# Fold and Newton step of the row norms on GpSimd, and a new order of VectorE's work within each pair

## The chip, the cores and the metric

The kernel runs on one core of one Trainium2 chip. The metric is the device time of one execution in microseconds (us). The core has five engines that work side by side, each through its own queue in order: TensorE (PE; its weight loads are shown apart as PEld), VectorE (DVE), ScalarE (ACT), GpSimd (POOL) and SyncE (SP), whose queue here issues the loads from memory. An instruction that waits for a semaphore holds up everything behind it in its own queue.

## The reference

```python
def rmsnorm(x, g):
    rms = np.sqrt(np.mean(x * x, axis=-1, keepdims=True) + 1e-06)
    return x / rms * g
q_n, k_n = rmsnorm(q, g_q), rmsnorm(k, g_k)         # (8, 12, 448, 64)
scores = q_n @ k_n^T / sqrt(64)
attn = softmax(scores) ; o = attn @ v               # heads joined: x is (3584, 768)
h = x @ w_in                                        # (3584, 1024)
solu = h * softmax(h)
ln = (solu - mean) / sqrt(var + 1e-06) * g_ln
out = ln @ w_out                                    # (3584, 768)
```

Eight sequences of 448 tokens with 12 heads of 64 go through attention with normalised q and k; the result goes through a feed-forward block of width 1024. The two weight matrices arrive as 64-bit floats and are turned into 32-bit floats on the chip.

## The kernel before

Work goes by pairs of heads: N = 48 pairs, n = 0 to 47, six to a sequence. The main loop (it begins after `load(3)` and `begin(0)`) runs over the pairs, and in the turn n it does pieces of several of them at once:

- **scores** (L598, L601): `scores(n, kc)` for kc = 0 to 3, each two halves of matmuls into PSUM tile `s`, and an exponential on ACT into `E`. The ring of `s` has two buffers, so the matmuls of a chunk wait for the exponential two chunks earlier.
- **values and sums** of the pair before: `values(n-1)` (L626, tile `o`) and `sums(n-1)` (L637, tile `sm`), the row sums of `E` by a matmul with ones. `add` forms the sums `es` that this matmul reads: for n < 12 two DVE additions (L612); from n = 12 one GpSimd addition (L615) and two DVE additions on top (L617).
- **divide(n-1)** (L650, L651, L652, L654): DVE turns the sums round, takes reciprocals and multiplies, which frees the buffers of `o` and `sm`. Its result goes to `xT`.
- **the norms of coming pairs**: `squares(n+3)` on ACT (L537), `row_sums(n+3)` on DVE (L542), `swap_sums(n+3)` (four GpSimd copies, L551), `fold_sums` (L555), `rsqrt_seed(n+2)` (three short ACT steps, L562 to L564), `rsqrt_step(n+2)` (a Newton step of three instructions on 128x28 elements, L568 to L570), `normalise(n+2)` on GpSimd (L575, tile `qkn`, one buffer), `qk_transpose(n+1)` on DVE (L585, tile `qkT`) and `gain(n+1)` on ACT (L589).
- **weights**: `convert_w` of one or two of 28 pieces a turn up to n = 21, in four stages that `step()` issues: low bits on ACT (L464, L465), high bits on DVE (L468, L469), join on DVE (L473), and for `w_out` a product on ACT (L478). `load_next` loads the piece three further on into one of three buffers `raw` (L449); it needs the buffer that the high and low bits have read.
- **feed-forward**: from n = 13 one event a turn, and from n = 23 up to four: `ff_in` (L669, tile `h`, one buffer), `ff_transpose` (L713), `ff_out` (L724). `ff_max` (L679, L682), `ff_moments` (L687 to L697, with one GpSimd power L697) and `ff_norm` (L701) follow an `ff_in` some units later. The rest of the events run after the loop.

`unit(f)` issues a piece of PE's work and then whatever `later` has put off to that place. The order within each engine is the order of the code; no scheduler changes it. The names in a DVE row of the trace read out<-in.

Of the kernel before, what the change touches and what calls it, by code (L numbers as in the profile page):

```python
# [14 lines left out]
OP = AluOpType  # L15
# [351 lines left out]
def fast_path(  # L367
# [17 lines left out]
    nc = tc.nc  # L385
# [11 lines left out]
    W_IN = 12  # L397
# [47 lines left out]
    def load_w(step):  # L445
        src, _, c, cols = step
        n = cols.stop - cols.start
        raw = work.tile([P, n, 2], U32, tag="raw", name="raw", bufs=3)
        nc.sync.dma_start(  # L449
            raw.rearrange("p n t -> p (n t)"),  # L450
            src[c * P : (c + 1) * P, :].bitcast(U32)[:, 2 * cols.start : 2 * cols.stop],
        )
        return raw
# [62 lines left out]
    def load(n):  # L516
        b, hp = divmod(n, NP)
        h0 = 2 * hp
        d = st[n] = {}
        d["qk"] = loads.tile([P, 2, NB, 32], FP32, tag="qk", name="qk", bufs=3)  # L520
        for s, src in enumerate((q, k)):
            for g in range(4):
                nc.sync.dma_start(
                    d["qk"][g * 32 : g * 32 + 32, s],
                    src[b, h0 + g // 2].rearrange("(b t) (x d) -> x t b d", t=32, x=2)[g % 2],
                )
# [7 lines left out]
    def squares(n):  # L534
        d = st[n]
        d["sq"] = work.tile([P, 2 * NB, 32], FP32, tag="sq", name="sq", bufs=1)
        nc.scalar.activation(d["sq"], d["qk"].rearrange("p s b d -> p (s b) d"), AF.Square)  # L537

    def row_sums(n):
        d = st[n]  # L540
        d["part"] = small.tile([P, 2 * NB], FP32, tag="part", name="part")
        nc.vector.tensor_reduce(d["part"], d["sq"], AX, OP.add)  # L542
# [3 lines left out]
    def swap_sums(n):  # L546
        d = st[n]
        d["ss"] = small.tile([P, 2 * NB], FP32, tag="ss", name="ss")
        for g in range(4):
            o = g ^ 1  # L550
            nc.gpsimd.tensor_copy(d["ss"][g * 32 : g * 32 + 32], d["part"][o * 32 : o * 32 + 32])  # L551

    def fold_sums(n):
        d = st[n]
        nc.vector.tensor_tensor(d["ss"], d["ss"], d["part"], OP.add)  # L555

    def rsqrt_seed(n):

        d = st[n]
        d["x"] = small.tile([P, 2 * NB], FP32, tag="nx", name="nx")  # L560
        d["y"] = small.tile([P, 2 * NB], FP32, tag="ny", name="ny")
        nc.scalar.activation(d["y"], d["ss"], AF.Ln, scale=1.0 / D, bias=eps)  # L562
        nc.scalar.activation(d["x"], d["ss"], AF.Copy, scale=-0.5 / D, bias=-0.5e-6)
        nc.scalar.activation(d["y"], d["y"], AF.Exp, scale=-0.5)  # L564

    def rsqrt_step(n):
        x, y = st[n]["x"], st[n]["y"]
        nc.vector.tensor_tensor(x, x, y, OP.mult)  # L568
        nc.vector.tensor_tensor(x, x, y, OP.mult)
        nc.vector.scalar_tensor_tensor(y, x, 1.5, y, OP.add, OP.mult)  # L570

    def normalise(n):
        d = st[n]
        d["qkn"] = work.tile([P, 2 * NB, 32], FP32, tag="qkn", name="qkn", bufs=1)
        nc.gpsimd.tensor_tensor(  # L575
            d["qkn"],
            d["qk"].rearrange("p s b d -> p (s b) d"),
            d["y"].rearrange("p b -> p b ()").to_broadcast([P, 2 * NB, 32]),
            OP.mult,
        )  # L580
# [10 lines left out]
    def scores(n, kc):  # L591
        d = st[n]
        if kc == 0:
            d["E"] = work.tile([SP, NJ, 2, S], FP32, tag="E", name="E")
        s = ps_t.tile([SP, 2, 512], FP32, tag="t", name="s")
        for h in range(2):
            hh = slice(h * D, (h + 1) * D)
            nc.tensor.matmul(  # L598
                s[:, h, 0:S], d["qkT"][hh, 1, kc * SP : (kc + 1) * SP], d["qkT"][hh, 0, :], start=True, stop=True
            )  # L600
        nc.scalar.activation(d["E"][:, kc], s[:, :, 0:S], AF.Exp)  # L601
# [5 lines left out]
    def add(n, kc):  # L607
        d = st[n]
        two = n < W_IN
        if kc in (1, 3) and two:  # L610
            d["es", kc] = work.tile([SP, 2, S], FP32, tag="es", name="es")
            nc.vector.tensor_tensor(d["es", kc], d["E"][:, kc - 1], d["E"][:, kc], OP.add)  # L612
        elif kc == 1:
            d["es", 3] = work.tile([SP, 2, S], FP32, tag="es", name="es")
            nc.gpsimd.tensor_tensor(d["es", 3], d["E"][:, 0], d["E"][:, 1], OP.add)  # L615
        elif not two:
            nc.vector.tensor_tensor(d["es", 3], d["es", 3], d["E"][:, kc], OP.add)  # L617
# [127 lines left out]
    def unit(f):  # L745
        nonlocal now
        f()
        now += 1
        due = [x for x in todo if x[0] <= now]
        todo[:] = [x for x in todo if x[0] > now]  # L750
        for _, g in sorted(due, key=lambda x: x[0]):
            g()
# [7 lines left out]
    stages = []  # L760

    def load_next():
        if len(raws) < len(wq):
            raws.append(load_w(wq[len(raws)]))
# [13 lines left out]
    def step():  # L778
        for c in stages:
            c.pop(0)()  # L780
# [5 lines left out]
    def second(t, a, b):  # L786
        return [(W_OUT + 1, lambda: ff_transpose(t)), a, (W_OUT + 1, lambda: ff_out(t, 0)), b, (W_OUT + 1, lambda: ff_out(t, 1))]

    nothing = (0, None)
    for t in range(NT):  # L790
# [4 lines left out]
        if len(waiting) > (LAG if t < NT - 8 else 1):  # L795
            c, _, d, _, e = second(waiting.pop(0), nothing, nothing)
# [6 lines left out]
    N = B * NP  # L803
# [7 lines left out]
    with tc.manual_schedule():  # L811
        for n in range(2):
            squares(n)
            row_sums(n)
            swap_sums(n)
            fold_sums(n)
            rsqrt_seed(n)
            rsqrt_step(n)
            normalise(n)
            if n == 0:  # L820
                qk_transpose(0)
                gain(0)
        squares(2)
        row_sums(2)
        swap_sums(2)
        load(3)
        begin(0)
        at = 0
        for n in range(N):
            due = []  # L830

            while at < len(events) and len(due) < (4 if n > W_OUT else 1) and events[at][0] <= n:
                due.append(events[at][1])
                at += 1

            def ff(k):
                for f in due[len(due) * k // 3 : len(due) * (k + 1) // 3]:
                    unit(f)


            unit(lambda: scores(n, 0))
            if n:
                add(n - 1, 3)
            if n + 1 < N:
                qk_transpose(n + 1)
            if n + 2 < N:
                fold_sums(n + 2)
            unit(lambda: scores(n, 1))
            step()
            ring = "o"  # L850
            ff(0)

            if n:
                unit(lambda: values(n - 1))
            if n >= W_IN:
                add(n, 1)
            if n + 2 < N:
                rsqrt_seed(n + 2)
            if n + 3 < N:
                squares(n + 3)  # L860
            if n + 4 < N:
                load(n + 4)
            if n + 2 < N:
                rsqrt_step(n + 2)
                normalise(n + 2)
            if n + 3 < N:
                row_sums(n + 3)
            step()
            for _ in stages:
                load_next()  # L870
            if n:
                unit(lambda: sums(n - 1))
                later(1, lambda n=n: divide(n - 1))
            if n + 1 < N:
                load_v(n + 1)
            if n + 3 < N:
                swap_sums(n + 3)
            step()
            begin(n + 1)
            if n + 1 < N:  # L880
                gain(n + 1)
            ring = "t"
            ff(1)

            unit(lambda: scores(n, 2))
            unit(lambda: scores(n, 3))
            add(n, 1 if n < W_IN else 2)
            ring = "o"
            ff(2)
        add(N - 1, 3)  # L890
        unit(lambda: values(N - 1))
        unit(lambda: sums(N - 1))
        divide(N - 1)
        ring = "t"

        last = events[at:]
        assert len(last) > len(wq) + 1
        again = [load_w(wq[x]) for x in range(2)]
        for x, (_, f) in enumerate(last):
            unit(f)  # L900
            if x < len(wq):
                check_w(x, again[x])
                if x + 2 < len(wq):
                    again.append(load_w(wq[x + 2]))
            if x == len(wq) + 1:
                check_all()
        for _ in range(4):
            unit(lambda: None)
# [73 lines left out]
```

## Time and profile before

| what | value |
|---|---|
| three runs | 1070.37, 1071.86, 1073.26 us (median 1071.86) |
| the profiled execution | 1071.4 us, of which 1069.6 us are the span from its first to its last instruction |
| PE busy | 998.1 us (93%) |
| DVE busy | 623.6 us (58%) |
| ACT busy | 379.3 us (35%) |
| POOL busy | 232.1 us (22%) |
| SP queue (q1) | 58.23 MB in 230016 packets |

The page cuts the span into 40 slices and gives each engine's busy share of a slice in tenths. The timeline lists start, length, engine, line, operation and out<-in, with the idle time of the engine just before in brackets and what ended it. The list of waits has: engine, what waited, what it waited for, us in total, number of times, the longest. The length of a matmul group is from its first start to the modelled end of its last.

### The profile page before, as it was taken

Reading aid. Unit: us, or ns where it says so; the run is one execution under the profiler, and the core shown is the slowest. Engines: PE = TensorE matmul, PEld = TensorE weight load, DVE = VectorE, ACT = ScalarE, POOL = GpSimd, SP = SyncE. Lnnn points to the kernel's source line nnn. Section 1 sums busy time; section 2 is a strip of 40 time slices with the busy share of each in tenths; the row PEclk is TensorE's granted clock in tenths of the full one; section 3 lists DMA queues with packets and bytes.
Section 4 is the critical chain, followed back from the end, with each engine's and each line's share of the span. In section 5 each row is a group of like instructions: output and inputs, shape, how many; then the busy total and the mean of one; then the engine's idle time right before and its main releaser. Section 6 shows DMA issues by size and latency. Waiting matters only on the chain.

```text
span 1069.6 us, 10556 instructions
## 1 busy us (share of the span) xinstructions
PE 998.1 (93%) x3571; PEld 446.4 (42%) x3571; DVE 623.6 (58%) x1013; ACT 379.3 (35%) x645; POOL 232.1 (22%) x314
## 2 busy tenths in 40 slices
PE   2988878898899999999999999999999999999997
PEld 0332323233244444444444444444444444455554
DVE  3999988888874355545454555444555443556430
ACT  4777754565533233323323233223322322111110
POOL 3322334324321122212131222112221111000000
PEclk9999989898999999999999999999999999999999
DMA  7756643343221111111221211211110002043330
GB/s 150 159 124 135 122 97 85 67 96 78 39 43 41 41 40 41 41 26 40 50 54 35 47 32 29 52 41 41 41 40 9 24 25 82 35 133 113 118 119 34
DMA packets 234426, 70.10 MB, mean 66 GB/s; under 512 B 223600, under 2 KB 223608, under 8 KB 234360
## 3 DMA queue, kind: packets, MB, share of 16 engines
q1 hardware_dynamic: 230016, 58.23, 25.2%
q10 hardware_dynamic: 4344, 11.08, 2.6%
q8 instruction: 30, 0.49, 0.2%
q14 instruction: 36, 0.29, 0.1%
HBM read 58.27 MB, written 11.01 MB: 65 GB/s over the span
## 4 chain that ended last, share of the span: by engine, by line
PE 69%; DVE 17%; ACT 7%; issue 3%; SPq 1%; DMA 0%; POOL 0%; ACTq 0%; DVEq 0%
PE po L724 28%; PE h L669 23%; PE o L626 7%; PE s L598 7%; DVE part L542 2%; DVE qkT L585 2%; PE sm L637 2%; PE pu L713 2%; DVE es L612 2%; ACT E L601 1%; DVE es L617 1%; DVE tmp L473 1%; DVE tmp L469 1%; DVE w_in L473 1%; DVE ss L555 1%
## 5 line engine op out<-in xcount | busy, mean ns | idle before, releaser
L669 PE MATMUL h<-w_in,xT 128*128 128x512 f32 x672 | 302.2, 599 | 0.0
L724 PE MATMUL po<-w_out,uT 128*128 128x384 f32 x896 | 299.4, 490 | 2.1 <-ACT uT L714 2.1
L724 PEld LDWEIGHTS po<-w_out,uT 128*128 128x128 f32 x896 | 167.4, 190 | 134.9 <-issue 14.5
L598 PE MATMUL s<-qkT 64*112 64x448 f32 x768 | 181.2, 590 | 44.0 <-ACT E L601 29.6
L601 ACT ACTIVATE E<-s 112x896 f32<-112x896 f32 x192 | 165.6, 911 | 87.0 <-PE s L598 86.8
L669 PEld LDWEIGHTS h<-w_in,xT 128*128 128x128 f32 x672 | 123.9, 190 | 164.2 <-issue 158.8
L626 PE MATMUL o<-E,v 112*64 112x448 f32 x768 | 156.3, 549 | 2.6 <-ACT uT L714 2.6
L697 POOL TENSOR_TENSOR he<-he,mhalf 128x1 f32<-128x1 f32 x28 | 22.0, 785 | 485.7 <-DVE he L696 392.4
L598 PEld LDWEIGHTS s<-qkT 64*112 64x112 f32 x768 | 61.8, 180 | 153.9 <-issue 64.9
L617 DVE TENSOR_TENSOR es<-es,E 112x896 f32<-112x896 f32 x72 | 80.2, 1114 | 57.5 <-ACT E L601 55.6
L575 POOL TENSOR_TENSOR qkn<-qk,ny 128x896 f32<-128x896 f32 x48 | 83.2, 1733 | 127.8 <-issue 71.7
L725 ACT COPY y<-po 128x384 f32<-128x384 f32 x56 | 26.8, 479 | 230.9 <-PE po L724 224.3
L615 POOL TENSOR_TENSOR es<-E 112x896 f32<-112x896 f32 x36 | 76.6, 2128 | 143.5 <-ACT E L601 129.7
L715 DVE COPY uT<-pu 128x512 f32<-128x512 f32 x28 | 19.3, 690 | 149.5 <-ACT uT L714 86.9
L626 PEld LDWEIGHTS o<-E,v 112*64 112x64 f32 x768 | 51.3, 138 | 100.8 <-issue 85.1
L682 ACT ACTIVATE u<-h,hmax 128x1024 f32<-128x1024 f32 x28 | 31.2, 1113 | 160.2 <-DVE hmax L679 160.2
L679 DVE TENSOR_REDUCE hmax<-h 128x1 f32<-128x1024 f32 x28 | 34.3, 1223 | 80.9 <-PE h L669 80.9
L637 PE MATMUL sm<-es,ones 112*64 112x448 f32 x240 | 56.1, 564 | 11.4 <-DVE es L617 10.2
L542 DVE TENSOR_REDUCE part<-sq 128x28 f32<-128x896 f32 x48 | 52.0, 1083 | 8.4 <-ACT sq L537 7.8
L551 POOL COPY ss<-part 32x28 f32<-32x28 f32 x192 | 50.0, 260 | 21.2 <-DVE part L542 12.3
L585 DVE STREAM_TRANSPOSE qkT<-qkn 128x896 f32<-128x896 f32 x48 | 53.0, 1104 | 1.9 <-POOL qkn L575 1.9
L687 DVE TENSOR_TENSOR u<-h,u 128x1024 f32<-128x1024 f32 x28 | 34.3, 1224 | 31.5 <-ACT u L682 31.3
(66 smaller groups left out, 637.2 us busy)
## 6 DMA issues: line engine op xcount, KB each, us to landing
raw<-in_moe_w_in_dram SPq DMA_DIRECT2D x24, 512.0 KB, 4.1
raw<-in_moe_w_out_dram SPq DMA_DIRECT2D x32, 384.0 KB, 3.3
qk<-in_q_dram SPq DMA_DIRECT2D x192, 56.0 KB, 2.4
qk<-in_k_dram SPq DMA_DIRECT2D x192, 56.0 KB, 2.3
v<-in_v_dram SPq DMA_DIRECT2D x48, 224.0 KB, 3.1
out_dram<-y ACTq DMA_DIRECT2D x28, 384.0 KB, 2.3
grow<-in_g_q_dram ACTq DMA_DIRECT2D x2, 0.2 KB
grow<-in_g_k_dram ACTq DMA_DIRECT2D x2, 0.2 KB
```

Of the source, the lines that this page charges most:

```text
L542: nc.vector.tensor_reduce(d["part"], d["sq"], AX, OP.add)
L551: nc.gpsimd.tensor_copy(d["ss"][g * 32 : g * 32 + 32], d["part"][o * 32 : o * 32 + 32])
L575: nc.gpsimd.tensor_tensor(d["qkn"], d["qk"].rearrange("p s b d -> p (s b) d"), d["y"].rearrange("p b -> p b ()").to_broadcast([P, 2 * NB, ...
L585: nc.vector.transpose(d["qkT"].rearrange("p s t -> p (s t)"), d["qkn"].rearrange("p b d -> p (b d)"))
L598: nc.tensor.matmul(s[:, h, 0:S], d["qkT"][hh, 1, kc * SP : (kc + 1) * SP], d["qkT"][hh, 0, :], start=True, stop=True)
L601: nc.scalar.activation(d["E"][:, kc], s[:, :, 0:S], AF.Exp)
L615: nc.gpsimd.tensor_tensor(d["es", 3], d["E"][:, 0], d["E"][:, 1], OP.add)
L617: nc.vector.tensor_tensor(d["es", 3], d["es", 3], d["E"][:, kc], OP.add)
L626: nc.tensor.matmul(d["o"][h * D : (h + 1) * D, :], d["v"][:, h, kc], d["E"][:, kc, h], start=(kc == 0), stop=(kc == NJ - 1),)
L637: nc.tensor.matmul(d["sm"][h * D : (h + 1) * D, :], ones[0:SP, :], es[:, h], start=(i == 0), stop=(i == len(tiles) - 1),)
L669: nc.tensor.matmul(d["h"][:, hs], xTs[m][:, c, i * P : (i + 1) * P], w_in[:, c, hs], start=(c == 0), stop=(c == KD - 1))
L724: nc.tensor.matmul(po, d["uT"][:, c], w_out[:, c, hs], start=(c == 0), stop=(c == KF - 1))
```

## The change

Two things are done. The fold (one instruction a pair) and the Newton step go from DVE to GpSimd. [...] And the order in a turn of the loop becomes another: the weight pieces' high bits and join stand ahead of `qk_transpose`, the next loads of raw weights follow at once, the swap and the fold of pair n+3 stand straight behind its row sums, and GpSimd's part of `es` stands behind those.

```diff
     def fold_sums(n):
         d = st[n]
-        nc.vector.tensor_tensor(d["ss"], d["ss"], d["part"], OP.add)
+        nc.gpsimd.tensor_tensor(d["ss"], d["ss"], d["part"], OP.add)
...
     def rsqrt_step(n):
         x, y = st[n]["x"], st[n]["y"]
-        nc.vector.tensor_tensor(x, x, y, OP.mult)
-        nc.vector.tensor_tensor(x, x, y, OP.mult)
-        nc.vector.scalar_tensor_tensor(y, x, 1.5, y, OP.add, OP.mult)
+        nc.gpsimd.tensor_tensor(x, x, y, OP.mult)
+        nc.gpsimd.tensor_tensor(x, x, y, OP.mult)
+        nc.gpsimd.tensor_scalar(x, x, 1.5, None, OP.add)
+        nc.gpsimd.tensor_tensor(y, x, y, OP.mult)
...
         swap_sums(2)
+        fold_sums(2)
         load(3)
...
             if n:
                 add(n - 1, 3)
+            unit(lambda: scores(n, 1))
+            step()
+            step()
+            for _ in stages:
+                load_next()
             if n + 1 < N:
                 qk_transpose(n + 1)
-            if n + 2 < N:
-                fold_sums(n + 2)
-            unit(lambda: scores(n, 1))
-            step()
             ring = "o"
             ff(0)
...
-            if n >= W_IN:
-                add(n, 1)
             if n + 2 < N:
                 rsqrt_seed(n + 2)
...
             if n + 3 < N:
                 row_sums(n + 3)
+                swap_sums(n + 3)
+                fold_sums(n + 3)
+            if n >= W_IN:
+                add(n, 1)
             step()
-            for _ in stages:
-                load_next()
...
-            if n + 3 < N:
-                swap_sums(n + 3)
-            step()
             begin(n + 1)
```

PE's instructions stand in the same order as before. In the changed kernel every line from 571 on has moved down by one (L585 is L586 there, and so on).

DVE, one turn of the early loop (n = 3, attention and weights only), before; it begins with the two additions `es` of the pair before:

```order
L612 TENSOR_TENSOR es<-E 112x896 x2
L585 STREAM_TRANSPOSE qkT<-qkn 128x896
L555 TENSOR_TENSOR ss<-ss,part 128x28
L468 TENSOR_SCALAR tmp<-raw 128x512
L469 SCALAR_TENSOR_TENSOR tmp<-raw,tmp 128x512
L568 TENSOR_TENSOR nx<-nx,ny 128x28
L569 TENSOR_TENSOR nx<-nx,ny 128x28
L570 SCALAR_TENSOR_TENSOR ny<-nx,ny 128x28
L542 TENSOR_REDUCE part<-sq 128x28
L473 TENSOR_TENSOR w_in<-tmp 128x512
L650 STREAM_TRANSPOSE r<-sm 128x448
```

The same place in the changed kernel:

```order
L613 TENSOR_TENSOR es<-E 112x896 x2
L468 TENSOR_SCALAR tmp<-raw 128x512
L469 SCALAR_TENSOR_TENSOR tmp<-raw,tmp 128x512
L473 TENSOR_TENSOR w_in<-tmp 128x512
L586 STREAM_TRANSPOSE qkT<-qkn 128x896
L542 TENSOR_REDUCE part<-sq 128x28
L651 STREAM_TRANSPOSE r<-sm 128x448
```

The four short instructions are gone, the three weight instructions stand together ahead of the transpose, and the row sums follow the transpose.

GpSimd, one turn from n = 12 on, before, with the first row of the next; `he` is the power of `ff_moments`, which every second turn has:

```order
L697 TENSOR_TENSOR he<-he,mhalf 128x1
L615 TENSOR_TENSOR es<-E 112x896
L575 TENSOR_TENSOR qkn<-qk,ny 128x896
L551 COPY ss<-part 32x28 x4
L615 TENSOR_TENSOR es<-E 112x896
```

The same turn in the changed kernel:

```order
L698 TENSOR_TENSOR he<-he,mhalf 128x1
L568 TENSOR_TENSOR nx<-nx,ny 128x28
L569 TENSOR_TENSOR nx<-nx,ny 128x28
L570 TENSOR_SCALAR nx<-nx 128x28
L571 TENSOR_TENSOR ny<-nx,ny 128x28
L576 TENSOR_TENSOR qkn<-qk,ny 128x896
L551 COPY ss<-part 32x28 x4
L555 TENSOR_TENSOR ss<-ss,part 128x28
L616 TENSOR_TENSOR es<-E 112x896
```

Five short instructions have come in, and `es` has gone from the front of the turn to its end, behind the normalisation, the copies and the fold.

SP's queue, one early turn and the start of the next, before:

```order
L523 DMA qk<-in_q_dram 32x14x32 x4
L523 DMA qk<-in_k_dram 32x14x32 x4
L449 DMA raw<-in_moe_w_in_dram 128x1024
L532 DMA v<-in_v_dram 112x8x64
L523 DMA qk<-in_q_dram 32x14x32 x4
```

and in the changed kernel:

```order
L449 DMA raw<-in_moe_w_in_dram 128x1024
L523 DMA qk<-in_q_dram 32x14x32 x4
L523 DMA qk<-in_k_dram 32x14x32 x4
L532 DMA v<-in_v_dram 112x8x64
L449 DMA raw<-in_moe_w_in_dram 128x1024
```

The raw weights, which wait for DVE's high bits of this turn, are now issued ahead of the turn's q and k.

## The prediction

> **What bounds the kernel now.** First the page's slices of PE, a window of the early pairs and one behind them (columns: window, length, then busy us with count for PE, PEld, DVE, ACT, POOL; granted clock, DMA share, GB/s), and the list of PE's waits up to 134 us (first row) and from 134 to 325 us (the others):
>
> ```profile
> PE   2988878898899999999999999999999999999997
> 54.00:81.00 27.00, 24.42 (x120) 8.45 (x120) 26.20 (x46) 19.38 (x33) 7.84 (x15) 1.00 0.59 123
> 134.00:160.00 26.00, 19.43 (x74) 7.08 (x72) 22.17 (x33) 15.06 (x25) 9.84 (x12) 0.87 0.47 99
> PE s L598 <- ACT E L601: 15.8, 13, 4.0
> PE s L598 <- ACT E L601: 13.8, 7, 6.6
> PE sm L637 <- DVE es L617: 10.2, 4, 2.9
> ```
>
> From about the twelfth slice PE is full to the end: there nothing is to be had. Before that there are two stages with room: pairs without feed-forward up to 134 us (**stage A**), where DVE is busy 26.2 of 27 us, and pairs with one `ff_in` up to about 300 us (**stage B**), where PE waits and its granted clock falls to 0.87. One period of stage A, from the timeline:
>
> ```profile
> 79.45 1.09 DVE L542 TENSOR_REDUCE part<-sq 128x28 f32<-128x896 f32 x1
> 79.52 1.70 POOL L575 TENSOR_TENSOR qkn<-qk,ny 128x896 f32<-128x896 f32 x1 [6.22 <-issue]
> 80.45 1.31 DVE L473 TENSOR_TENSOR w_in<-tmp 128x512 uint32<-128x512 uint32 x1
> 80.67 0.65 ACT L589 ACTIVATE qkT<-qkT,gcol 128x448 f32<-128x448 f32 x1
> 81.22 1.70 ACT L601 ACTIVATE E<-s 112x896 f32<-112x896 f32 x2
> ...
> 83.86 2.08 DVE L612 TENSOR_TENSOR es<-E 112x896 f32<-112x896 f32 x2
> 83.92 3.23 PE L626 MATMUL o<-E,v 112*64 112x448 f32 x16
> 85.86 1.10 DVE L585 STREAM_TRANSPOSE qkT<-qkn 128x896 f32<-128x896 f32 x1
> 86.89 0.15 DVE L555 TENSOR_TENSOR ss<-ss,part 128x28 f32<-128x28 f32 x1
> 86.95 0.42 DVE L468 TENSOR_SCALAR tmp<-raw 128x512 uint32<-128x512 uint32 x1
> 86.97 1.67 PE L637 MATMUL sm<-es,ones 112*64 112x448 f32 x8
> 87.41 0.69 DVE L469 SCALAR_TENSOR_TENSOR tmp<-raw,tmp 128x512 uint32<-128x512 uint32 x1
> 88.02 0.18 DVE L568 TENSOR_TENSOR nx<-nx,ny 128x28 f32<-128x28 f32 x1
> 88.58 1.76 PE L598 MATMUL s<-qkT 64*112 64x448 f32 x8
> 88.70 1.09 DVE L542 TENSOR_REDUCE part<-sq 128x28 f32<-128x896 f32 x1
> ```
>
> The period is 88.70 - 79.45 = 9.25 us, and DVE has no gap in it: DVE bounds stage A. PE alone could turn in 3.05 (o to sm) + 1.61 (sm to s) + two times 1.76 (s) = 8.2 us.
>
> **What contention costs DVE.** The same join without a normalisation beside it, four copies that met it, and a pair of rows of stage B:
>
> ```profile
> 26.86 0.68 DVE L473 TENSOR_TENSOR w_in<-tmp 128x512 uint32<-128x512 uint32 x1
> 27.08 2.02 POOL L551 COPY ss<-part 32x28 f32<-32x28 f32 x4 [0.18 <-DVE part L542]
> 160.21 2.31 POOL L615 TENSOR_TENSOR es<-E 112x896 f32<-112x896 f32 x1 [6.59 <-ACT E L601]
> 160.56 2.00 DVE L568 TENSOR_TENSOR nx<-nx,ny 128x28 f32<-128x28 f32 x1
> ```
>
> The join takes 0.68 us alone and 1.31 beside `qkn`, and a Newton instruction of 0.18 us takes 2.00 when it comes during GpSimd's `es`: it stands until that ends, at 162.52. The row sums, which read one tensor, show nothing of the kind: beside `qkn` at 79.45 they last 1.09, no longer than the transpose of as many elements at 85.86 without it (1.10). So the order matters as much as the moved work.
>
> **The change, part by part: stage A.** DVE loses the three Newton instructions, 88.70 - 88.02 = 0.68 us. The fold saves nothing in start times: the transpose ends at 86.96, the high bits start at 86.95. The join ahead of the transpose runs before the normalisation, which cannot start until the transpose has emptied the single `qkn`: 1.31 - 0.68 = 0.63 less. It now follows at once the instruction whose result it reads, which costs 0.12 (the pair 468 and 469 shows 0.04 of delay behind the end, where independent neighbours overlap by 0.08). DVE's period: 9.25 - 0.68 - 0.63 + 0.12 = 8.06.
>
> A second chain stands close by. `gain` and with it the exponentials of chunks 2 and 3 wait for the transpose, and PE's next `s` and `o` for those. From o's start to the transpose's end DVE would need 2.0 (es) + 0.46 + 0.73 + 0.60 (weights) + 1.10, less 0.06, = 4.83; then gain 0.65, two exponentials 1.70, the last half of s 0.9: 8.1. Both give about 8.1, and so does PE alone (8.2).
>
> What is added is five short GpSimd instructions a pair. No row shows one of 128x28 there; the nearest (min/median/max in ns):
>
> ```profile
> L551 POOL COPY ss<-part x192: 196/201/981, 9.7 to 835.9; 32x28 f32<-32x28 f32 x192
> L697 POOL TENSOR_TENSOR he<-he,mhalf x28: 547/548/1329, 176.4 to 1010.3; 128x1 f32<-128x1 f32 x28
> ```
>
> I bound one by 0.20 (a copy with as many columns) and 0.55 (a power), and take 0.30, near the copy: 28 columns at the 1.9 ns of `qkn` add 0.05, and a wait on its own predecessor a few hundredths. GpSimd then has 1.70 + 1.27 + 5 x 0.30 = 4.5 us of work in a period of over 8, so its own time is hidden. What isn't hidden is that the step (ready with ACT's seed, which needs no fold of this turn any more: the last exponential ends some 0.9 us after o's start, then three short ACT steps, so about 1.6) falls beside DVE's es, high bits and join. The cost to DVE lies between 0 (GpSimd always stands back, as the copies at 27.08 did behind the join: 2.02 us for four, which take 0.92 at 636.34 in a row below) and 4 x 0.30 = 1.2 (each gets in ahead of a DVE instruction). It can get in where DVE itself waits for its own result, behind 468 and 469; I take 0.3, nearer to the copies. Period 8.4, and ten periods of 9.25 in stage A: 10 x 0.85 = **8.5 us gained**, bounds 10 x 0 and 10 x 1.15.
>
> SP: raw weights now leave ahead of q and k, and wait for 469.
>
> ```profile
> 27.11 0.41 SPq L449 DMA_DIRECT2D raw<-in_moe_w_in_dram  x1
> 31.08 2.12 SPq L523 DMA_DIRECT2D qk<-in_k_dram  x4
> qk<-in_k_dram SPq DMA_DIRECT2D x192, 56.0 KB, 2.3
> ```
>
> Where raw (and v) stood ahead, the last k was issued 33.20 - 27.11 = 6.1 us later and landed 2.3 after that: 8.4. From 469's end, 3.1 us behind o, that is 11.5; the squares of the next turn would start 8.4 + 1.6 = 10.0 behind o, and can be 0.9 late, since ACT then waits for the transpose anyway. It is 0.6 beyond that, over two turns of the loop: 0.3 a period at worst. I cost it at nothing, since v now stands behind; the cover is thin.
>
> **Stage B.** PE's rows, the first and last `o` of it among them:
>
> ```profile
> 129.92 3.23 PE L626 MATMUL o<-E,v 112*64 112x448 f32 x16
> 142.92 3.33 PE L598 MATMUL s<-qkT 64*112 64x448 f32 x8 [6.58 <-ACT E L601]
> 158.98 3.23 PE L626 MATMUL o<-E,v 112*64 112x448 f32 x16
> 171.62 3.23 PE L626 MATMUL o<-E,v 112*64 112x448 f32 x16
> 177.29 1.76 PE L637 MATMUL sm<-es,ones 112*64 112x448 f32 x4 [2.45 <-DVE es L617]
> 205.69 3.23 PE L626 MATMUL o<-E,v 112*64 112x448 f32 x16
> 221.92 1.82 PE L598 MATMUL s<-qkT 64*112 64x448 f32 x8 [1.35 <-ACT E L601]
> 297.65 3.23 PE L626 MATMUL o<-E,v 112*64 112x448 f32 x16 [0.47 <-ACT uT L714]
> ```
>
> The first and the last o enclose eleven intervals, 297.65 - 129.92 = 167.7 us. PE without a wait takes 171.62 - 158.98 = 12.64. Two kinds of wait stand in it. **Waits for E**: ACT does the weight product (behind the join), the next low bits and `gain` before chunk 2, and the join came late in DVE: behind transpose, fold, Newton and row sums, one of them held up by `es` for up to 1.8 us. After the change the join comes some 3 us earlier, `es` runs beside divide, whose four instructions read at most one tensor from SBUF, as the row sums do, and these waits go. **Waits for es** (four): h, its maximum, exponential, product and moments stand ahead of the second addition in DVE. That chain is untouched. After either wait PE runs at half speed (3.33 for 1.76 at 142.92).
>
> So after: the first interval, a stage A turn with a product (0.6) and a second piece's low bits (1.2), 8.4 + 1.8 = 10.2; five without a wait at 12.64; four with an es wait, from the third such: 221.92 + 1.75 - 205.69 - 1.35 = 16.63 (half speed included); the last, without `ff_in`, about 9.0. Sum 10.2 + 63.2 + 66.5 + 9.0 = 148.9: **18.8 us gained**. Bounds: 10 (es late, below) and 25 (the half speed behind the four waits goes too).
>
> GpSimd's `es` now runs behind the transpose by 1.70 + 0.92 + 0.30 + 2.1 = 5.0 us; the DVE addition that waits for it has hmax, moments and the copies of uT behind it. It is due when h ends, and by my count of DVE's work comes 0.2 us before that: no cost, but the cover is 0.2.
>
> **The prologue.** Norms of pairs 0 and 1 lie on the way to the first matmuls: five times 0.30 for four DVE instructions of some 0.19 is 0.7 more each; part hides behind loads. I take 0.8 lost, bounds 0 and 2.
>
> **From 300 us on** PE is full. `es` is later by the normalisation, copies and fold:
>
> ```profile
> 636.34 0.92 POOL L551 COPY ss<-part 32x28 f32<-32x28 f32 x4
> 642.26 1.09 DVE L617 TENSOR_TENSOR es<-es,E 112x896 f32<-112x896 f32 x1 [4.17 <-ACT E L601]
> ```
>
> The copies end at 637.26, the fold 0.3 and es 2.1 later: 639.7, and DVE wants it at 642.26, because the exponential isn't ready sooner. 2.6 us of cover: nothing lost.
>
> **Sum.** From the profiled execution's 1071.4 us, which is 0.5 below the median shown: + 0.8 - 8.5 - 18.8 gives **1044.9 us**.
>
> [...]
>
> **The rivals.**
> - [...] If each step instruction gets in ahead of a DVE one, the period is 8.06 + 1.2 = 9.26, stage A gains nothing, and the time is 1053.4. For it: 160.56. Against: the copies at 27.08.
> - *es comes late.* If GpSimd's five microseconds become six or more, the addition holds hmax up; four times up to 2.1 us (one `es`): 1044.9 + 8.4 = 1053.3. For it: the cover of 0.2.
> - *More is gained.* If contention costs nothing and the es waits shrink enough that PE keeps its clock behind them (1.6 each, by 3.33 for 1.76): 1044.9 - 2.5 - 6.4 = 1036.
> - *Slower.* The later `es` breaks the full stage. If the 2.6 us of cover go, DVE holds the copies of uT and hmax, and every second of 25 pairs costs a wait like 177.29's (2.45) and half speed (1.6): 12 x 4.05 = 49, so 1094. It decides from a GpSimd instruction of over 0.30 + 2.6/5 = 0.8 us; the row of 0.55 speaks against.
> [...]
>
> **How the numbers follow.** My forecast 1044.9 (say 1040 to 1050) gets 0.52; the two rivals around 1053 together 0.23; more gained 0.13; the same 0.05; slower 0.07. The range reaches from 1036 to 1060: from the deeper gain past both middle rivals, with what they would give half together. Measurement tells 0.3% (3.2 us) from no change: faster 0.88, same 0.05, slower 0.07.
>
> **What would show it.** Right: the join at 0.68 in every early pair, the period of DVE's row sums near 8.4, no Newton lines on DVE, no long instructions on DVE beside `es` but L618, PE's waits for E in stage B below 3 us in all, four es waits left, the time behind 325 us unchanged. Wrong: short GpSimd instructions over 0.5 us, L618 waiting for GpSimd's es with hmax behind it, squares waiting for q or k in stage A, or new PE waits behind 325 us.

## The result and the profile after

The changed kernel takes 1045.11 us (median; 1043.77 to 1045.45), the kernel before 1072.56 beside it: a ratio of 0.9744, 95% interval 0.9725 to 0.9763. The profiled execution took 1045.33 us, 1043.4 of them span. The forecast of 1044.9 was met. Its terms were off by up to 3 us each, as is shown below, and made up for one another.

The page's slices of PE, then the two windows shown before (window, length, busy us with count for PE, PEld, DVE, ACT, POOL; granted clock, DMA share, GB/s), then PE's waits: the first row up to 134 us, the others from 134 to 325 us.

```profile
PE   2899999899999999999999999999999999999997
```

```profile
54.00:81.00 27.00, 26.20 (x130) 9.05 (x128) 24.99 (x35) 20.91 (x35) 14.01 (x32) 1.00 0.67 149
134.00:160.00 26.00, 26.00 (x102) 9.71 (x100) 18.89 (x27) 15.79 (x28) 13.77 (x23) 1.00 0.49 107
```

```profile
PE s L599 <- ACT E L602: 10.4, 14, 3.8
PE sm L638 <- DVE es L618: 9.9, 4, 3.4
PE s L599 <- ACT E L602: 0.5, 2, 0.3
```

In the early window PE is now the busiest engine (26.20 of 27 us, where DVE had 26.20 before). In the second it has no gap and its clock stays at 1.00. Behind 134 us the waits for E are all but gone (0.5 us); the four for es are still there.

Where the time went can be read from the starts of PE's o, one for each pair. The table cuts every kernel of this study at the same four rows: from the first squares (ACT L537) to the first o; eleven intervals to the twelfth o (stage A); one to the thirteenth; ten to the 23rd (with the one before, stage B); and the rest. The time before the first squares, in which the first loads run, is left out: it was 7.2 to 7.5 us in the profiles of the first two kernels and 9.3 to 9.5 in all others, whatever their code.

| kernel | to the first o | 11 intervals | usual interval | the 12th | 10 intervals | rest | ratio to before (95%) |
|---|---|---|---|---|---|---|---|
| before | 22.81 | 99.62 | 9.25 | 16.26 | 151.47 | 771.95 | 1 |
| the change | 26.05 | 92.98 | 8.43 | 8.44 | 137.37 | 771.39 | 0.9744 (0.9725 to 0.9763) |
| order_alone | 25.18 | 107.49 | 9.81 | 11.38 | 144.42 | 771.63 | 0.9972 (0.9961 to 0.9983) |
| move_alone | 24.82 | 93.33 | 8.43 | 11.01 | 151.56 | 770.40 | 0.9908 (0.9891 to 0.9926) |
| fold_only | 24.64 | 92.77 | 8.43 | 8.73 | 139.05 | 770.74 | 0.9754 (0.9738 to 0.9770) |
| step_only | 26.57 | 107.40 | 9.81 | 11.33 | 150.41 | 772.33 | 1.0049 (1.0032 to 1.0066) |
| fold_old_order | 23.06 | 97.54 | 9.10 | 17.24 | 150.55 | 770.42 | 0.9969 (0.9957 to 0.9982) |
| dve_extra | 26.19 | 94.08 | 8.43 | 8.44 | 135.83 | 771.44 | 0.9745 (0.9729 to 0.9762) |
| pool_extra | 28.37 | 99.04 | 9.20 | 11.12 | 137.51 | 771.75 | 0.9861 (0.9844 to 0.9878) |
| join_late | 25.64 | 93.81 | 8.43 | 14.53 | 141.96 | 770.66 | 0.9843 (0.9824 to 0.9863) |
| es_before_copies | 25.74 | 93.30 | 8.43 | 8.44 | 133.87 | 770.53 | 0.9708 (0.9692 to 0.9725) |
| prologue_old | 23.96 | 92.77 | 8.43 | 8.43 | 136.44 | 770.85 | 0.9725 (0.9709 to 0.9741) |
| both_better | 22.35 | 92.77 | 8.43 | 8.43 | 133.87 | 770.63 | 0.9685 (0.9669 to 0.9701) |
| best_step_dve | 22.58 | 92.75 | 8.43 | 9.25 | 133.43 | 770.48 | 0.9689 (0.9673 to 0.9705) |

The change lost 3.2 us up to the first o and gained 6.6 in stage A, 7.8 and 14.1 in stage B and 0.6 behind it; with 0.3 from the loads that is the 26.2 by which the span shrank. Stage B as a whole, before and after (columns as in the two windows above, PE alone):

```profile
129.92:297.65 167.73, 143.14 (x518) 0.92 0.36 77
126.20:272.01 145.81, 134.56 (x518) 0.98 0.43 90
```

PE was idle for 24.6 us of it before and for 11.3 after, so 13.3 of the 21.9 us gained are less waiting. Nearly all of the rest is clock: before, 27.3 us of the stage ran at half speed, after 6.8, and by that PE's work took 11.6 and 3.3 us longer than at full speed. One period of stage A after, from the timeline (start, length, engine, line, operation, out<-in; in brackets the idle time just before and what ended it):

```profile
75.61 3.23 PE L627 MATMUL o<-E,v 112*64 112x448 f32 x16
76.13 0.43 DVE L468 TENSOR_SCALAR tmp<-raw 128x512 uint32<-128x512 uint32 x1
76.60 0.69 DVE L469 SCALAR_TENSOR_TENSOR tmp<-raw,tmp 128x512 uint32<-128x512 uint32 x1
77.18 0.25 POOL L568 TENSOR_TENSOR nx<-nx,ny 128x28 f32<-128x28 f32 x1 [3.42 <-ACT ny L564]
77.33 0.69 DVE L473 TENSOR_TENSOR w_in<-tmp 128x512 uint32<-128x512 uint32 x1
77.50 0.62 POOL L569 TENSOR_TENSOR nx<-nx,ny 128x28 f32<-128x28 f32 x1
77.93 1.10 DVE L586 STREAM_TRANSPOSE qkT<-qkn 128x896 f32<-128x896 f32 x1
78.57 0.24 POOL L571 TENSOR_TENSOR ny<-nx,ny 128x28 f32<-128x28 f32 x1
78.66 1.67 PE L638 MATMUL sm<-es,ones 112*64 112x448 f32 x8
80.27 1.76 PE L599 MATMUL s<-qkT 64*112 64x448 f32 x8
80.39 0.65 DVE L651 STREAM_TRANSPOSE r<-sm 128x448 f32<-128x448 f32 x1 [0.38 <-PE sm L638]
80.93 0.92 POOL L551 COPY ss<-part 32x28 f32<-32x28 f32 x4
82.29 1.82 PE L599 MATMUL s<-qkT 64*112 64x448 f32 x8 [0.27 <-ACT E L602]
82.56 2.08 DVE L613 TENSOR_TENSOR es<-E 112x896 f32<-112x896 f32 x2
```

The high bits of the next pair start 8.43 later. DVE now has a gap of 0.38 in the period, ended by PE; PE's only gap is 0.27, ended by the exponential. So PE (8.16 of its own) and the ring of exponentials bound stage A. DVE's own work is 8.43 - 0.38 = 8.05 us. Side by side with DVE it is GpSimd that takes longer: its L569 takes 0.61 to 0.64 beside the join, in ten pairs, and 0.24 without one (35.11 and 128.46).

### The profile page after: what moved, and what is told of

Same layout as the page of the kernel before. It is cut to its first block, busy times and chain, and to the rows that moved or that the text cites. A ratio compares the mean times of both kernels' runs of the same rounds, so it can differ in the third digit from the quotient of the medians.

```text
span 1043.4 us, 10599 instructions
## 1 busy us (share of the span) xinstructions
PE 991.1 (95%) x3571; PEld 445.0 (43%) x3571; DVE 541.4 (52%) x821; ACT 378.3 (36%) x645; POOL 293.9 (28%) x554
## 3 DMA queue, kind: packets, MB, share of 16 engines
q1 hardware_dynamic: 230016, 58.23, 25.7%
HBM read 58.27 MB, written 11.01 MB: 66 GB/s over the span
## 4 chain that ended last, share of the span: by engine, by line
PE 85%; ACT 5%; DVE 4%; POOL 2%; SPq 1%; issue 1%; DMA 1%; ACTq 0%; POOLq 0%; DVEq 0%
PE po L725 28%; PE h L670 26%; PE s L599 12%; PE o L627 12%; PE sm L638 4%; ACT E L602 3%; PE pu L714 2%; SPq L523 1%; DVE es L618 1%; POOL qkn L576 1%; POOL es L616 1%; ACT uT L715 1%; DMA raw<-in_moe_w_out_dram 1%; DVE bs L692 0%; POOL ss L551 0%
## 5 line engine op out<-in xcount | busy, mean ns | idle before, releaser
L599 PE MATMUL s<-qkT 64*112 64x448 f32 x768 | 177.2, 579 | 25.6 <-ACT qkT L590 12.3
L618 DVE TENSOR_TENSOR es<-es,E 112x896 f32<-112x896 f32 x72 | 78.4, 1088 | 82.0 <-ACT E L602 44.3
L680 DVE TENSOR_REDUCE hmax<-h 128x1 f32<-128x1024 f32 x28 | 34.2, 1223 | 85.3 <-PE h L670 85.3
L568 POOL TENSOR_TENSOR nx<-nx,ny 128x28 f32<-128x28 f32 x48 | 14.2, 295 | 191.7 <-ACT ny L564 191.7
L586 DVE STREAM_TRANSPOSE qkT<-qkn 128x896 f32<-128x896 f32 x48 | 53.0, 1103 | 5.2 <-POOL qkn L576 5.2
```

Source lines behind the costliest of these rows:

```text
L586: nc.vector.transpose(d["qkT"].rearrange("p s t -> p (s t)"), d["qkn"].rearrange("p b d -> p (b d)"))
L599: nc.tensor.matmul(s[:, h, 0:S], d["qkT"][hh, 1, kc * SP : (kc + 1) * SP], d["qkT"][hh, 0, :], start=True, stop=True)
```

## The experiments

### Which part of the change carries it

order_alone takes the new order but leaves fold and step on DVE; move_alone takes the old order with both on GpSimd.

```diff
 order_alone, against the changed kernel
-        nc.gpsimd.tensor_tensor(d["ss"], d["ss"], d["part"], OP.add)
+        nc.vector.tensor_tensor(d["ss"], d["ss"], d["part"], OP.add)
...
                 qk_transpose(n + 1)
+            if n + 2 < N:
+                fold_sums(n + 2)
...
                 swap_sums(n + 3)
-                fold_sums(n + 3)
 (the step is the three DVE instructions of before)
```

> Fold and Newton step stay on VectorE, everything else in the new order. Theory (the order carries most of the gain): VectorE gets its 0.68 us a pair back, so its period in the early pairs is about 8.06 + 0.68 = 8.75 instead of the 8.43 measured after the change: 3.2 us lost over ten periods. The prologue gets back up to 2.9 us. The normalisation starts some 0.7 us later, so GpSimd's es is later by as much and the four waits for es grow. Time 1045 to 1053, about 1049; join still 0.69 us each. Rival (the moved work carries it): VectorE is too slow again behind the weights, PE's waits for E between 134 and 300 us are back near the 13.8 us of before, and the time is 1058 or more.

```diff
 move_alone, against the kernel before
-        nc.vector.tensor_tensor(d["ss"], d["ss"], d["part"], OP.add)
+        nc.gpsimd.tensor_tensor(d["ss"], d["ss"], d["part"], OP.add)
 (the step is the four GpSimd instructions of the change)
```

> Fold and Newton step on GpSimd, old order. Theory (order): the join stays beside the normalisation at about 1.3 us, VectorE's other two-input instructions still stand behind GpSimd's es for about 2 us once a turn, and the weight product still waits for the join. Early period 8.57 to 8.75, prologue up to 1 us slower, PE's waits for E in the pairs with one ff_in still over 7 us: time 1056 to 1064. Rival (moved work): VectorE relieved of 0.68 us and of the fold's waits is enough, 1052 or less.

order_alone took 1071.07 us beside 1074.23, move_alone 1063.84. The moves came out as expected; the order alone did not: it gains 0.3%, where 1045 to 1053 had been expected. By themselves the parts give 3 and 10 us, together 27. In order_alone stage A became slower than before (9.81 a pair). Its trace (the fold, ACT's seed, and gain):

```profile
76.51 0.15 DVE L555 TENSOR_TENSOR ss<-ss,part 128x28 f32<-128x28 f32 x1
76.69 0.32 ACT L562 ACTIVATE ny<-ss,eps 128x28 f32<-128x28 f32 x1 [2.69 <-DVE ss L555]
79.52 0.65 ACT L589 ACTIVATE qkT<-qkT,gcol 128x448 f32<-128x448 f32 x1
```

The fold stands in DVE's queue behind the three weight instructions and the transpose. ACT waits 2.69 us for its 0.15 us, and the seed, the squares, the low bits and gain queue up behind. The o of this pair started at 72.97, so gain comes 6.55 us behind o, and PE's next s waits 1.64 for its exponential. (In the kernel before, ACT waited for the fold as well, 19.7 us in ten pairs of stage A. What that was worth there, fold_old_order shows below.) So the theory became: the new order needs the fold out of DVE's queue and early; the step matters little. Two kernels divide the moves:

```diff
 fold_only, against the changed kernel (the fold stays on GpSimd)
-        nc.gpsimd.tensor_tensor(x, x, y, OP.mult)
-        nc.gpsimd.tensor_tensor(x, x, y, OP.mult)
-        nc.gpsimd.tensor_scalar(x, x, 1.5, None, OP.add)
-        nc.gpsimd.tensor_tensor(y, x, y, OP.mult)
+        nc.vector.tensor_tensor(x, x, y, OP.mult)
+        nc.vector.tensor_tensor(x, x, y, OP.mult)
+        nc.vector.scalar_tensor_tensor(y, x, 1.5, y, OP.add, OP.mult)
```

> The new order with the fold on GpSimd straight behind the copies; the step's three instructions stay on DVE, between the transpose and the row sums. My theory after the first four runs: the new order needs the fold out of DVE's queue and early, because there it stands behind weights and transpose, and ACT's seed, squares, low bits and gain queue up behind it. Then this kernel keeps nearly all: DVE has 8.06 + 0.68 = 8.74 us in a pair without feed-forward, over the 8.43 of the whole change, so ten times 0.3 is lost, and the two stages behind go as in the whole change. 1046 to 1050 us beside 1072 to 1074 before, ratio 0.975 to 0.979, seed not waiting for the fold. Rival: both moves are needed (the step on DVE waits for ACT's seed and holds the row sums up): period 9.3 or more, 1058 us or more, ratio 0.986 or more.

```diff
 step_only, against order_alone
 (the step is the four GpSimd instructions of the change)
```

> The new order with the step on GpSimd and the fold on DVE at its old place behind the transpose. My theory (the fold decides): ACT's seed still waits 2.7 us for the fold, gain comes as late as with the order alone, the period stays at 9.3 to 9.8; 1063 to 1071 us, ratio 0.990 to 0.997. Rival (the step decides, since DVE waits there for ACT): period 8.4 to 8.7, 1045 to 1050 us, ratio 0.974 to 0.979.

fold_only took 1047.13 us beside 1073.59, step_only 1078.88, slower than before. The fold decides; its engine and its place in the order went together here, and no run separates the two. In fold_only:

```profile
74.74 0.24 POOL L555 TENSOR_TENSOR ss<-ss,part 128x28 f32<-128x28 f32 x1
77.11 0.31 ACT L562 ACTIVATE ny<-ss,eps 128x28 f32<-128x28 f32 x1
79.97 0.65 ACT L589 ACTIVATE qkT<-qkT,gcol 128x448 f32<-128x448 f32 x1
```

The fold is done 2.1 us before ACT comes to the seed, and gain starts 79.97 - 76.18 = 3.79 us behind o. I had expected a period of 8.74 here. PE's is 8.43; DVE has no gap and turns in 8.50 (L469 starts at 68.95 and at 77.45), so the step costs it 0.45 a pair, and it falls behind PE by 0.07 a pair, which does not reach PE in the eleven intervals. The fold by itself in the old order:

```diff
 fold_old_order, against the kernel before
-        nc.vector.tensor_tensor(d["ss"], d["ss"], d["part"], OP.add)
+        nc.gpsimd.tensor_tensor(d["ss"], d["ss"], d["part"], OP.add)
```

> The old order with the fold alone on GpSimd; the step stays on DVE. By my prediction the fold saves nothing in start times, and the 0.82 us a pair that the two moves together save without feed-forward come from the step: period 9.1 to 9.25 there, 1068 to 1075 us, ratio 0.995 to 1.001. Rival: the fold on GpSimd matters in the old order too, as it does in the new one: period 8.9 or less, ratio 0.993 or less.

It took 1069.97 us beside 1073.36. The period went from 9.25 to 9.10, by the fold's own 0.15; with the step gone too (move_alone) it is 8.43, and the twelfth interval falls from 17.24 to 11.01. ACT's wait for the fold is 0.16 in fold_old_order (103.33), where it was 2.1 before: shortening it gained nothing there, because DVE still has no gap. In the old order the step's 0.67 is what counts, and the fold next to nothing; in the new order it is the other way round.

### What bounds stage A now

```diff
 dve_extra, against the changed kernel, in row_sums
+        if 3 <= n < W_IN + 3:
+            more = small.tile([P, 8], FP32, tag="more", name="more")
+            nc.vector.tensor_reduce(more, d["sq"][:, 0:8], AX, OP.add)
```

> The whole change with one more DVE reduction (128x256 elements to 128x8, some 0.35 us) behind the row sums in each of twelve early pairs. If DVE no longer bounds the pairs without feed-forward (PE and the ring of exponentials do), the period stays at 8.43 and DVE's wait for sm shrinks from 0.38 to about 0: 0 to 1 us lost, ratio 0.973 to 0.976. If DVE bounds them still, as my prediction had it (8.06 and contention), the period grows by the whole 0.35 to 8.8: 3 to 4 us lost, ratio 0.977 to 0.979.

1046.41 us beside 1073.59, period 8.43. The added instruction took 0.41, and r started 0.46 behind it without a wait:

```profile
83.31 0.41 DVE L545 TENSOR_REDUCE more<-sq 128x8 f32<-128x256 f32 x1
83.77 0.65 DVE L654 STREAM_TRANSPOSE r<-sm 128x448 f32<-128x448 f32 x1
```

DVE has some 0.4 us to spare in a pair, as its gap said. GpSimd's spare time was tested in the same way:

```diff
 pool_extra, against the changed kernel, behind the step
+        more = small.tile([P, 2 * NB], FP32, tag="more", name="more")
+        for _ in range(4):
+            nc.gpsimd.tensor_tensor(more, x, y, OP.mult)
```

> The whole change with four more short GpSimd instructions behind the step in every pair, some 1.3 us of GpSimd's time. By my prediction's covers: nothing in the pairs without feed-forward (period 8.43), nothing from 300 us on (2.6 us of cover there), and in the stage between es comes 1.3 later, with hmax behind it: the four waits for es grow by 1 to 1.3 each, and by half speed behind them: 4 to 9 us lost, ratio 0.978 to 0.983. Rival (the cover behind 300 us is thinner than I counted): new waits there, 12 us or more lost, ratio 0.985 or more. Rival (GpSimd costs nothing anywhere): ratio 0.974 to 0.976.

1059.0 us beside 1073.36: 12 to 13 us lost against the change, and not where I had looked. The ten intervals of stage B are 137.51 as with the change and the rest is the same, but the first o comes 2.3 us later, the twelfth interval is 11.12, and stage A has a period of 9.20 from its sixth interval on. The ratio lies where the second rival had it, for a reason that none of the three named:

```profile
71.55 3.97 POOL L551 COPY ss<-part 32x28 f32<-32x28 f32 x4
71.55 2.09 DVE L616 TENSOR_TENSOR es<-E 112x896 f32<-112x896 f32 x2
75.87 0.32 ACT L562 ACTIVATE ny<-ss,eps 128x28 f32<-128x28 f32 x1 [1.82 <-POOL ss L555]
```

In the changed kernel the copies end at 81.85 and DVE's two-input addition es begins at 82.56: 0.7 us apart. Pushed 1.3 us back they meet it and the weight instructions behind it, and four copies take 3.97 us instead of 0.92. The fold behind them is late, and ACT waits for it as in order_alone. So GpSimd's path to the fold has 0.7 us of cover, where the prediction set 4.5 us of work against a period of over 8 and called its time hidden.

### What took the waits out of stage B

```diff
 join_late, against the changed kernel
             step()
-            step()
             for _ in stages:
                 load_next()
...
             if n + 3 < N:
                 row_sums(n + 3)
+            step()
+            if n + 3 < N:
                 swap_sums(n + 3)
```

> The whole change, except that the weight join stands at its old place again, behind the row sums (and so beside the normalisation), with the product of w_out behind it. If the early join is what takes the waits for E out of the pairs with one ff_in (the product then stands in ACT ahead of the exponentials), most of the 14 us there come back, and the interval into that stage is 11 instead of 8.4: 1054 to 1062 us, ratio 0.983 to 0.990; the pairs without feed-forward keep a period of 8.43, since PE bounds them. Rival: the late es of GpSimd (no longer beside DVE's short instructions) is what helps there: ratio 0.974 to 0.977.

1057.52 us beside 1073.36, in the range expected if the early join is the cause, though the twelfth interval is 14.5 and not 11. Its rows at the entry of stage B, and PE's waits from 134 to 300 us:

```profile
135.82 0.61 ACT L478 ACTIVATE w_out<-tmp,gcol 128x384 f32<-128x384 f32 x1 [3.24 <-DVE tmp L473]
138.51 0.65 ACT L590 ACTIVATE qkT<-qkT,gcol 128x448 f32<-128x448 f32 x1
```

```profile
PE s L599 <- ACT E L602: 9.8, 5, 4.9
PE sm L638 <- DVE es L618: 8.3, 4, 2.3
```

ACT waits 3.24 us for the join before it can multiply, and low bits, gain and exponentials stand behind that. 6.1 us of the twelfth interval and 4.6 of the ten behind it come back, 10.7 of the 21.9 that stage B gained. PE's waits for E are 9.8 again (13.8 before), so the early join removes most of them; the other half of the gain comes with the rest of the change, and no run divides it further. Stage A loses nothing of note: its period stays 8.43, although the join takes 1.4 to 1.5 us there again beside qkn. The es waits were treated by putting GpSimd's es ahead of the copies:

```diff
 es_before_copies, against the changed kernel
                 row_sums(n + 3)
-                swap_sums(n + 3)
-                fold_sums(n + 3)
             if n >= W_IN:
                 add(n, 1)
+            if n + 3 < N:
+                swap_sums(n + 3)
+                fold_sums(n + 3)
```

> The change, with GpSimd's es ahead of the four copies and the fold instead of behind them. Theory (es comes late): the waits for es of 3.42 and 2.54 us come from es ending after h; 1.2 us earlier they fall to 2.0 like the other two, and the half speed behind the long one (1.6 to 3.2 us) goes: time 1039.5 to 1042. Rival: the feed-forward chain alone sets these waits, es only seems to end them: they stay, and the time stays at 1044 to 1046. Copies and fold come 2.1 us later in both; if that were late for the seeds, new waits for E of over 2 us in all would show.

1043.09 us beside 1074.23 (before stood 1.7 higher here than beside the change). The ten intervals shrink by 3.5: 2.0 of shorter waits, and 1.6 because one stretch of 3.41 us at half speed is left of two. In the changed kernel, two of the four es waits looked like the second of these two (the rows of PE; and DVE's L618 and L680 ahead of the second):

```profile
165.13 0.97 PE L638 MATMUL sm<-es,ones 112*64 112x448 f32 x4 [1.99 <-DVE es L618]
166.03 1.76 PE L599 MATMUL s<-qkT 64*112 64x448 f32 x8
...
186.62 1.09 DVE L618 TENSOR_TENSOR es<-es,E 112x896 f32<-112x896 f32 x1 [2.06 <-POOL es L616]
187.63 1.22 DVE L680 TENSOR_REDUCE hmax<-h 128x1 f32<-128x1024 f32 x1
...
194.43 1.76 PE L638 MATMUL sm<-es,ones 112*64 112x448 f32 x4 [3.42 <-DVE es L618]
196.12 3.33 PE L599 MATMUL s<-qkT 64*112 64x448 f32 x8
```

PE had gone on from h to s at 186.09; hmax started 1.54 later, behind an addition that had waited 2.06 for GpSimd. In es_before_copies all four waits are 1.99.

### The first pairs, and a better kernel

```diff
 prologue_old, against the changed kernel (pairs 0 to 2 fold and step on DVE; turn 0 in the old order)
-        nc.gpsimd.tensor_tensor(d["ss"], d["ss"], d["part"], OP.add)
+        eng = nc.vector if n < 3 else nc.gpsimd
+        eng.tensor_tensor(d["ss"], d["ss"], d["part"], OP.add)
...
 (the step likewise; in turn 0 the transpose and fold_sums(2) stand ahead of the high bits, the join behind row_sums)
```

> The change, but pairs 0 to 2 have fold and Newton step on VectorE and turn 0 stands in the old order. Theory: the first o came 2.9 us later after the change (33.22 for 30.30) because the norms of pairs 0 to 2 became slower, and copies and fold of pair 2 stood behind the weights; with it back the first o is at 30.3 and the time is 2.9 lower, about 1042. Rival: part of it is only shifted, since the first interval between two o was 8.66 after the change and 7.1 before and the ring of exponentials sets the pace from then on: then 1.4 to 1.6 is gained, 1043.6. Third: nothing, 1045.

1044.42 us beside 1074.23; from the first squares to the first o 23.96, against 25.7 to 26.2 in the change, es_before_copies and dve_extra, which run the first pairs alike. One profile places the first o only to some 1.6 us, though: both_better, below, runs the first pairs as prologue_old does and has 22.35. The s ahead of the first o starts at 30.06 in both and takes 3.32 at half speed in prologue_old, 1.82 in both_better. Alone, its ratio overlaps that of the change. With es ahead of the copies too (both edits above; both_better), and then with the step on DVE in every pair (best_step_dve: fold_only's edit on both_better):

> The first pairs' norms on DVE in the old order, and from then on GpSimd's es between the normalisation and the copies. If the two gains stand in different places of the program they add up: ratio 0.9744 - 0.002 - 0.0036 = 0.968 to 0.970, some 1039 to 1041 us. Rival: the first pairs gain nothing by themselves (their start is set by the loads), and it is no faster than es alone ahead of the copies: 0.9705 to 0.972.

> As both_better, but the Newton step on DVE for every pair: of the two moves only the fold is left. With the whole change the step on DVE cost about 1 us (1047.1 against 1045.1, ratio 0.9754 against 0.9744), so if the step's move is worth nothing of note, this kernel stands within 0.15% of both_better: ratio 0.968 to 0.970, 1039 to 1041 us, period 8.43 without feed-forward. Rival: without the whole change's slack in ACT's and GpSimd's order the three instructions on DVE push the row sums and the addition of es back: period 8.7 or more, or longer waits for es with one ff_in, ratio 0.972 or more.

both_better took 1039.64 us beside 1073.59 (0.9685), best_step_dve 1039.76 beside 1073.79 (0.9689). The two gains add up, and the Newton step's move is worth nothing that can be measured: the two intervals are almost the same.

## Why the prediction came out right, and where its steps did not

That the total came within 0.2 us is luck: the terms for stage A and the first pairs were too good by 1.9 and 2.4 us, the one for stage B too small by 3.1.

- **DVE bounded stage A: right.** DVE's own period after was worked out as 8.06 and is 8.05. The 0.3 of contention added to it was wrong (from 30 to 126 us DVE's high bits took 0.42 to 0.45 and 0.69 and its join 0.69 in every pair), but PE and the ring, which the prediction had at 8.2 without the wait of 0.27 for the exponential, end at 8.43. A period of 8.4 came out of the wrong bound.
- **"Ten periods of 9.25": too many.** The first two intervals of before were 8.43 and 8.44 and had nothing to give. The term of 8.5 us measured 6.6.
- **"The join out of contention", 0.63 a pair: not needed in stage A.** The join is at 0.69 us there, as forecast, but join_late keeps the period with the join at 1.4 to 1.5. It earns its place in stage B, through the weight product, with about half of what is gained there.
- **"The fold saves nothing in start times": the step that failed.** In the old order it was nearly right (0.15 a pair). In the new order the fold's move is the condition of the whole gain (0.9972 to 0.9754, 23 us), by how early ACT gets it, not by DVE's time. The prediction took the earlier seed for granted in a bracket and priced only the instruction. The step, priced at 0.68 a pair, is worth nothing that can be measured in the new order.
- **Waits for E go: right,** and stage B gained 21.9, not 18.8: the twelfth interval came to 8.44, not 10.2, so neither the product nor the second piece's low bits cost PE anything there, and the ten behind it to 137.4, not 138.7. That the raw loads ahead of q and k cost nothing was right too: in stage A no instruction of ACT waited for a load.
- **Four es waits stay: right in number.** Half speed followed one of them, not four: the next s took 3.33 at 196.12 and 1.76 behind the other three. But "the cover is 0.2" failed at two of the four: L618 waited for GpSimd's es with hmax behind it, a sign that the prediction had named as wrong. The rival that priced this at 8.4 for four was right in its mechanism and is worth 3.5. The four intervals were put at 66.5 and measured 15.23 + 19.41 + 14.84 + 15.40 = 64.9, close by two errors that offset each other: two longer waits, and half speed left out three times.
- **Short GpSimd instructions at 0.30: right.** 0.24 to 0.28 long, 0.32 from start to start at 77.18. **The prologue: mis-sized, outside its bounds.** 0.8 was forecast (0 to 2), 3.2 measured. The first norm is slower by 0.7, as worked out (first squares to first s 8.37 before, 9.10 after). What was left out is turn 0's new order: pair 2's copies meet DVE's high bits and join, and its seed is late. With both, the gain of pair 1 comes 1.9 us later (28.60 - 7.17 for 27.04 - 7.49). Another 1.4 is clock: the s ahead of the first o takes 3.18 at half speed after (30.11) and took 1.82 before (28.55).

Copies, fold and seed of pair 2, before; and the same after, with L469 beside the copies (the join follows at 24.41):

```profile
22.26 0.92 POOL L551 COPY ss<-part 32x28 f32<-32x28 f32 x4
23.22 0.19 DVE L555 TENSOR_TENSOR ss<-ss,part 128x28 f32<-128x28 f32 x1
23.83 0.32 ACT L562 ACTIVATE ny<-ss,eps 128x28 f32<-128x28 f32 x1
```

```profile
23.36 2.06 POOL L551 COPY ss<-part 32x28 f32<-32x28 f32 x4
23.61 0.69 DVE L469 SCALAR_TENSOR_TENSOR tmp<-raw,tmp 128x512 uint32<-128x512 uint32 x1
25.50 0.24 POOL L555 TENSOR_TENSOR ss<-ss,part 128x28 f32<-128x28 f32 x1
25.77 0.32 ACT L562 ACTIVATE ny<-ss,eps 128x28 f32<-128x28 f32 x1 [1.65 <-POOL ss L555]
```

- **Nothing behind 300 us: right** (771.95 and 771.39), and pool_extra, 1.3 us later there, has 771.75.

Not tried: the fold early on DVE, straight behind the copies, and the step alone in the old order.

## What to carry to other kernels

A short instruction is priced by who waits for it, not by its length: 0.15 us of fold, standing 2.7 us too late in a queue, undid an order that is worth 23 us. When an edit has several parts, undo each one in the new order and do each one in the old: here neither half showed what the whole does, and the half that looked like the bigger saving was worth nothing. A sum that comes out right can hide terms that are wrong in both directions; cut the trace at the same rows in both kernels and compare term by term.

## What the runs showed of the hardware that was not expected

- The same wait of PE, 1.99 us at sm, was followed by half speed at 210.91 in the kernel before (the next s took 3.05) and at 195.27 in es_before_copies, and by full speed (1.76) at 165.13 after and three times in es_before_copies. After 2.54 us at 253.08 after, the next s took 1.76 too. In the traces of before and after, from 100 to 1000 us, each stretch between two changes of the granted clock lasted 3.41 us or a whole multiple of it (6.83, 10.24, 17.07, 27.31, 30.72). Cut into pieces of 3.41 us at these changes, the two traces have seven pieces at full speed with 1.99 to 3.38 us of PE's idle time, and half speed followed each of them; eleven have 0.90 to 1.80, and it followed none. The 1.99 us at 195.27 in es_before_copies fell into one such piece; of the 1.99 us at 165.13 after, 1.72 did, and the 2.54 us were divided over two, as 1.63 and 0.91. The pieces lie differently in each trace: one begins at 190.92 before, at 194.14 after and at 193.29 in es_before_copies. So what a wait of some 2 us cost here was in part luck.
- In stage A of the changed kernel it is GpSimd that takes longer where the two engines overlap: a Newton instruction of 0.24 takes 0.62 beside DVE's join, while the join keeps its 0.69. Four copies, 0.92 in all (80.93), take 2.06 beside high bits and join (23.36), and 3.97 in pool_extra (71.55). In join_late it is DVE: its join starts 0.76 behind qkn (74.12 and 73.36) and takes 1.49.

Of es_before_copies, the wait of 1.99 with half speed behind it; then four of these pieces, two around the wait at 167.39, which full speed followed, and two around this one (window, length, PE busy us with count; granted clock, DMA share, GB/s):

```profile
195.27 0.97 PE L638 MATMUL sm<-es,ones 112*64 112x448 f32 x4 [1.99 <-DVE es L618]
196.17 2.85 PE L599 MATMUL s<-qkT 64*112 64x448 f32 x8
```

```profile
165.99:169.40 3.41, 2.01 (x10) 1.00 0.00 0
169.40:172.81 3.41, 3.41 (x11) 1.00 0.64 174
193.29:196.71 3.42, 1.44 (x8) 1.00 0.01 2
196.71:200.12 3.41, 3.41 (x10) 0.50 0.45 118
```

Both waits were 1.99 us. The first left PE busy for 2.01 us of its piece, the second for 1.44, and half speed followed the second alone.
